# Pooling of k and v by halvings, and a new order for the first 750 of 2,051 pieces

## The chip, the core and the metric

The kernel runs on one core of a Trainium2 chip. Its time is the device time of one execution, in microseconds (us). A core has a matrix engine (PE, whose weight loads are listed apart as PEld), a vector engine (DVE), an activation engine (ACT) and a general engine (POOL); each works through a queue of its own, in order. SP is the queue that issues the DMA transfers.

## What is computed

Attention over keys and values that are averaged by eight, then a block that turns the result by learned angles and mixes it over tokens and channels. Eight batches, eight heads of 64, 576 tokens:

```python
k_p = k.reshape(B, H, Sp, pool, D).mean(axis=3)      # B=8 H=8 S=576 D=64 pool=8 Sp=72
v_p = v.reshape(B, H, Sp, pool, D).mean(axis=3)
scores = scale * np.matmul(q, k_p.transpose(0, 1, 3, 2))
attn = np.exp(scores - scores.max(-1, keepdims=True))
attn = attn / (np.sum(attn, axis=-1, keepdims=True) + 1e-09)
x = (attn @ v_p) as [8, 576, 512]
theta = x @ w_theta
zr, zi = x * np.cos(theta), x * np.sin(theta)
y = np.einsum('ts,bsd->btd', w_tok_r, zr) + np.einsum('ts,bsd->btd', w_tok_i, zi)
u = x + y
out = u + np.maximum(u @ w_ch, 0.0)
```

## The kernel before

Everything is float32; matrix products that need it are done as three products of a high and a low part ("h" and "l" at the end of a name), so most operands are first cast (`zh`, `xh`, `WTh`) and then subtracted (`zl`, `xl`, `WTl`).

The work is written as some 470 generators, called streams, and a long string, SCHEDULE, that says in which order they are advanced by one piece each. A word of the string is the name of a stream, and at its end, where there is a choice, the engine of that piece: v for DVE, g for POOL, a for ACT. Since each engine works through its queue in order, this string sets the order on all of them. There are 2,051 words. Per batch b the streams are: k and v (load a part of k or v), K and V (pool that part, and with no part number lay out the result as `kpT` or `Vh`, `Vl`), Q (queries, transposed into `qT`), S (scores, softmax; `en` is the normed exponent), E (its transposition), X (attention output, into `xT`), T (the angles: `pt` is x times w_theta, then sine and cosine, into `z`), Z (cast and split z, into `zh` and `zl`), M (token mix, into `py`, added to `xT`) and F (channel product `pf` and the output). At the start come h (w_theta), w and W (token weights: convert, then transpose by PE from `wt` into `WTh` and `WTl`) and c (w_ch, into `chh` and `chl`). The weights arrive as float64 and are converted by `to_f32`: three scalings, a combination on DVE at L366, and an addition on POOL at L368.

One pooling adds, for every pooled key or value, eight rows of 64 numbers. A part j = 0 or 1 of k or v is a tile of 128 partitions by 1024 numbers (`kpst`, `vpst`), the part j = 2 one of 64 by 512 (`kprst`, `vprst`). Batch 0 is pooled by matrix products on PE. From batch 1 on, `pool_sum` does it, on DVE by one reduction (L471), on POOL by halvings: the first half plus the second, three times, until 64 numbers are left (on POOL an operation of 512 numbers or more is cut in two by `InHalves`, L190). The large tiles `kpst`, `vpst` and `wcts` of the converted w_ch share one buffer, so that the next part can be loaded only when the last is pooled. The first 750 words put 11 pools on DVE: K1.0, K1.1, V1.0, K1.2, V1.1, K2.2, V1.2, K2.0, V2.2, V2.1, V3.2. Later in the string come four more on DVE: V4.1, K5.0, V6.2, K7.1.

After the change the lines behind the removed branch have numbers lower by four.

Of the kernel before, what the change touches and what calls it, by code (L numbers as in the profile page):

```python
# [35 lines left out]
w1.0a S0.2 w1.1v X0.0.0 w1.0v X0.0.1 X0.0.3 w1.1a W0a w1.1v S0.2a Q1.0 X0.0.1a w1.0 S0.4 w1.1 S0.3 W0 Q1.1 Q1.0
X0.0.0a S0.4 w1.1v X0.0.2 w1.0g S0.3g X0.0.2v X0.0.3v T0.0g T0.1g Q1.1a k1.1 w2.0 K1.1v W1 w2.0a S0.4 T0.0v W0 S0.3g
w2.0v W1a T0.1g S0.3 Q1.0a S0.2 W1 T0.0 w2.1 S0.4v w3.0 S0.3a K1 v1.0 w2.1v w3.0v w2.0a w2.1a T0.0 S0.2a w2.0 T0.1
w3.1 Q1.2 W1 w2.1a S0.4v T0.0 K1a S0.3 S0.3a S0.4 k1.2 S0.4a S0.4 Q1.3 V1.0v S0.4a T0.0 W0a w2.1 w3.0v T0.1 T0.1 w3.1a
X0.2.1 K1.2v X0.2.2 w3.0v w3.1v T0.0 X0.2.3 w2.0g X0.2.2a W1a W0 w3.1v T0.0a X0.2.0 T0.0 w4.0 v1.1 w2.1g w3.1 w3.0  # L40
w3.1g Q1.4 T0.0 X0.2.1v W2 T0.0 X0.2.3a Q1.2 w4.0v V1.1v Q1.3 X0.2.0a T0.2g T0.1 T0.1 w4.0a T0.2v T0.1a W2a c0 T0.2
Q1.3a w4.0a W2 T0.3g X0.2.3g T0.1 T0.3g T0.2 c0a T0.1 T0.3 w3.0g Q1.2v W2 T0.2 T0.4g T0.1 T0.2 c0a W1 w4.0 c1 T0.2
T0.4g T0.3 W2v T0.2a T0.2 c0a T0.2 W2 T0.4 w4.0g T0.3 T0.3 T0.2 T0.3 T0.4 W3 c0 Q1.4 T0.3a c0g c0g T0.4 T0.3 T0.4 T0.3
T0.4 c0g W3a T0.4 T0.3 W4 W3 T0.4 K1 Z0.0g K1a c1a S1.0 c1a W4a W4 c1a S1.0 c1 M0.0.0 W4a W4 Z0.1g Q1.4v c1v Z0.0v c1v
Z0.1v S1.0 M0.1.0 W4a W4 M0.0.0 M0.0.0 k2.2 M0.1.0 c2 W3 M0.1.0 W4a S1.0 c1v W4 S1.0g K2.2v c2a W3a W3 v1.2 M0.0.0
S1.0g S1.1 c2a c2a S1.1 S1.0 S1.1 M0.0.1 c2 S1.0v S1.0 c2g V1v S1.0 M0.0.1 M0.0.1 c2v c3 c2v S1.0a M0.1.1 S1.1 c3a
V1.2v S1.1g S1.1g S1.0 V1g c3a Z0.2a c3v S1.2 S1.2 M0.1.1 M0.1.0 S1.1 V1 v2.2 S1.3 M0.0.1 c3 c3g M0.2.0 c3v M0.2.0
M0.1.1 Z0.2v V1g S1.1a S1.1 M0.2.0 c3v M0.1.0a M0.1.1 Q2.0 S1.2 S1.1 k2.0 S1.1a M0.2.0 S1.4 S1.2 V1g Z0.3g M0.2.1
S1.2a S1.1 Q2.0 X1.0.0 X1.0.0v S1.2v X1.0.2 X1.0.1 X1.0.1a X1.0.3 X1.0.3v M0.2.1 S1.3 Z0.3g S1.2 X1.0.2a T1.0g T1.0g
S1.2a M0.0.1g M0.2.0v K2.0v M0.0.0v M0.2.1 M0.2.1 S1.2 T1.0 Q2.0 M0.2.0g S1.2 S1.3 S1.3 S1.2a S1.4 S1.3g k2.1 S1.3g  # L50
V2.2v T1.0 M0.3.0 M0.3.0 M0.1.1a Q2.1 S1.3 K2.1g S1.2 S1.4 T1.0 M0.3.1 S1.3v S1.3 M0.2.1v M0.0.1v M0.0.0g S1.3 M0.3.1
S1.3a K2 M0.2.1g S1.4 M0.3.0 S1.4g T1.1v k3.2 K2a M0.3.1 S1.3 T1.0 M0.3.0 M0.3.1 S1.4v T1.0 K2 M0.3.1g S1.4 Q2.1 v2.0
T1.0a K2v S1.4v S1.4 T1.1g Q2.1 T1.0 S1.4 T1.0 T1.1 S2.0 T1.0 S1.4a S1.4 V2.0g X1.2.2 T1.1 T1.1 M0.1.1g M0.3.0a v2.1
X1.2.0 X1.2.2a M0.3.1g X1.2.1 M0.1.0g S2.0 X1.2.3 T1.1 T1.1 Q3.0 X1.2.0a X1.2.3v M0.3.0v X1.2.1a T1.1v S2.0 T1.2g
F0.0.1 T1.2v T1.1 X1.2.3g S2.0 K3.2g T1.2 S2.0g T1.1 T1.1 S2.0g S2.1 V2.1v T1.3a Q3.0 T1.2 T1.3g T1.2 F0.0.1 S2.1
F0.0.0 S2.0 F0.0.0 T1.2 T1.3 F0.1.1 T1.4g F0.0.1 T1.2 F0.0.0 F0.1.0 S2.1 k3.0 K3.0g T1.2a S2.1 T1.2 T1.2 T1.2 T1.4v
S2.1g V2a F0.1.0 S2.1v k3.1 F0.2.0 T1.3 T1.3 F0.1.1 S2.2 S2.1 T1.3 T1.3 V2g T1.3v F0.0.1 E2.0 T1.3 S2.2 E2.0 S2.4 T1.3
S2.2 T1.3 S2.2 T1.4 T1.4 K3.1g T1.4 E2.0 F0.2.1 S2.3 T1.4 T1.4 F0.1.1 v3.0 T1.4 F0.2.0 F0.3.1 F0.1.0 F0.3.0 T1.4 Q3.0
Z1.0a Z1.1g F0.3.1 S2.2a F0.2.1 S2.2v E2.0 F0.3.0 K3 S2.3 K3a S2.3 M1.1.0 Z1.1v Z1.0g Q3.1 M1.0.0 E2.0a S2.3 M1.0.0
M1.0.1 M1.0.0 V2 S2.2 V3.0g M1.0.0 M1.0.0a F0.3.1 S2.3v M1.0.1 E2.0a V2g M1.0.1 F0.3.0 M1.1.1 S2.3v E2.0g E2.0g M1.1.0  # L60
S2.4 M1.0.1 M1.1.0 F0.1.1 F0.2.1 V2g Q3.1 v3.2 S2.4 K3 S2.4 S2.3 K3a F0.2.0 F0.3.1 Q3.1 M1.1.1 Z1.3g M1.1.1 S2.4a
M1.0.1a X2.0.0 S2.4g M1.1.0 X2.0.1 S2.4 X2.0.3 X2.0.0a v3.1 X2.0.2 X2.0.1a Z1.2a Z1.3v S3.2 X2.0.3a S3.2 S3.3 X2.0.2a
T2.0g T2.0v M1.3.0 E2.2 S3.2 S3.2 S3.2v M1.1.0v Z1.2g T2.0 T2.0 E2.2 E2.2 M1.2.1 T2.0 T2.1a S3.2v M1.2.1 T2.0 M1.1.1
S3.3 V3.1g M1.1.0v M1.2.1 T2.0 E2.2 M1.2.0 S3.4 M1.2.0 S3.0 V3.2v S3.3 M1.2.1 M1.1.1g S3.3 M1.0.1g M1.3.1 T2.1v S3.2
M1.2.0 M1.2.1v E2.2a E2.2g E2.2g E2.2g S3.3a M1.3.1 S3.3v k4.2 M1.2.0 S3.4 M1.2.0a k4.0 M1.3.1 M1.1.1g K4.2g M1.3.0
X2.2.2 M1.3.1 T2.0a S3.4 M1.3.0 S3.3 F0.2.1 X2.2.2a S3.4 T2.0 S3.4v M1.3.0 X2.2.0 S3.4g M1.2.1g X2.2.3 Q4.0 S3.4
X2.2.1 M1.2.0g S3.0 S3.1 X2.2.0a S3.0 M1.3.1a Q4.0 T2.0 T2.0 M1.3.1v V3g X2.2.3a v4.2 V3v K4.0g X2.2.1a T2.1 F1.0.1
T2.1 S3.0 M1.0.0g M1.3.0a E3.2 T2.2g F1.1.1 T2.1 F1.0.1 F1.2.1 V3 E3.2 T2.2g T2.3a M1.3.0g T2.1 Q4.0 F1.1.1 T2.1 V3v
F1.0.0 T2.1v F1.0.1 F1.0.0 F1.1.0 F1.0.0 T2.2 F1.2.1 S3.0a k4.1 E3.2 S3.0g F1.1.0 E3.2 K4.1g T2.1 T2.3g T2.1 K4 F1.2.0
T2.1 E3.2g S3.1 E3.2a F1.1.0 T2.2 S3.1 E3.2g F1.1.1 F1.3.0 E3.2g T2.2 Q4.1 K4a T2.2 Q4.1 F1.3.1 T2.2 V3g S3.0 T2.2a  # L70
S3.1 F1.3.0 F1.2.0 K4 T2.2 Q4.1 T2.2 K4a F1.0.1 T2.2 F1.3.1 F1.3.0 F1.3.1 T2.3 T2.3 T2.3 F1.1.1 F1.2.1 F1.2.0 X3.2.2
X3.2.3 X3.2.3a X3.2.1 S3.1g X2.2.3g X3.2.0 S4.2 X3.2.2v T2.3 X3.2.1v V4.2g X3.2.0a T2.3 S3.1v X3.2.3v T2.3a T2.4g
T2.4g S4.0 S3.1 T2.3 T2.3 T2.4 T2.3 T2.4 Z2.0v S4.0 T2.4 v4.0 T2.4 Z2.0g T2.4 Q5.0 F1.3.1 Z2.0g Z2.0g T2.4a E3.0 T2.4
M2.0.0 T2.4 T2.4 S4.0 Z2.1a S4.0 E3.0 S4.1 M2.0.1 Z2.1v E3.0 V4.0g M2.0.1 E3.0 M2.0.1 Z2.0g M2.0.0 Z2.0g S4.0a M2.0.0
S4.0v M2.0.0 M2.0.1 M2.1.0 M2.1.1 S4.1 M2.0.0 E3.0a E3.0g E3.0g M2.1.1 Z2.3a E3.0v M2.0.1 M2.1.1 M2.1.0 M2.1.0 M2.1.1
S4.0 X3.0.3 Z2.3g Z2.2a X3.0.0 X3.0.2 v4.1 X3.0.3a M2.3.0 V4.1v M2.1.0 M2.3.0 S4.1 X3.0.1 M2.3.0 X3.0.1v Z2.2g M2.2.0
S4.1 X3.0.2v M2.3.0 S4.1g k5.0 X3.0.0a k5.2 T3.4v Q5.0 S4.1v S4.3 T3.0g T3.0g S4.2 M2.2.0 S4.1 V4a T3.0 K5.0v T3.2a
S4.2 T3.0 k5.1 T3.1v T3.1g M2.2.0 T3.0 M2.1.0v M2.1.1a T3.1 M2.2.0 T3.0 F1.2.1 K5.2g E4.0 M2.3.1 T3.0 M2.3.1 S4.2
T3.0a M2.1.0v T3.0 M2.2.0a S4.2g S4.2v T3.0 v5.2 M2.0.0a M2.2.1 M2.3.1 T3.0 T3.2g T3.1 S4.4 M2.1.1v M2.3.0v T3.1 K5.1g
T3.1 M2.2.1 E4.0 E4.0 M2.2.0v E4.0 V4g T3.2 M2.0.0g M2.3.0g T3.1 S4.3 M2.0.1a T3.1a T3.1 T3.3a S4.3 T3.1 M2.3.1 T3.1  # L80
# [1164 lines left out]
```

## Time and profile before

| what | value |
|---|---|
| median of 3 runs | 562.17 us (560.41 to 565.18) |
| the profiled execution | 560.23 us |
| its span | 558.4 us |
| clock granted to PE, mean over the span | 0.993 of full |
| PE busy, PEld busy | 541.2 us, 511.7 us |
| DVE, ACT, POOL busy | 457.6, 331.8, 355.7 us |

The span is the time from the first to the last instruction that the profile shows; the execution's own time has 1.8 us around it. A matrix instruction is a weight load (PEld) and a product (PE), and loads run ahead under products. Both are shown, and in a stretch where PE has work all the time PEld is busy all the time too.

### The profile page before, as it was taken

What the parts mean: (1) busy time and instruction counts of PE and PEld (TensorE: products, weight loads), DVE (VectorE), ACT (ScalarE), POOL (GpSimd) and SP (SyncE); (2) the same over time, 40 slices, a digit from 0 to 9 for tenths busy, and PEclk for the clock granted to TensorE, in tenths of its full rate; (3) what the DMA queues carried; (4) which work ended last, traced back from release to release, by engine and by line L of the source; (5) the groups of instructions that cost most, each with busy time, mean ns of one, the idle gap of its engine ahead of it and who ended that gap; (6) DMA issues with size and microseconds to landing.
All of it is one profiled execution on the core that took longest, in us unless ns stands there. A gap on an engine that the chain in (4) does not pass through costs nothing.

```text
span 558.4 us, 11489 instructions
## 1 busy us (share of the span) xinstructions
PE 541.2 (97%) x4031; PEld 511.7 (92%) x4031; DVE 457.6 (82%) x850; ACT 331.8 (59%) x757; POOL 355.7 (64%) x497
## 2 busy tenths in 40 slices
...
GB/s 272 248 290 203 95 49 79 135 119 112 97 137 132 130 127 101 118 88 111 95 118 129 100 147 76 60 78 120 43 50 103 70 45 1 63 29 22 0 24 127
DMA packets 231802, 57.84 MB, mean 104 GB/s; under 512 B 218689, under 2 KB 220353, under 8 KB 231745
## 3 DMA queue, kind: packets, MB, share of 16 engines
...
## 4 chain that ended last, share of the span: by engine, by line
PE 66%; DVE 15%; ACT 8%; issue 4%; SPq 2%; DMA 2%; POOL 2%; DVEq 0%; POOLq 0%; ACTq 0%
PE py L1031 29%; PE pf L1064 12%; PE pt L943 11%; PE s L701 4%; PE pv L896 4%; PE px L957 2%; SPq L851 1%; PE warm L309 1%; DMA eraw<-G 1%; DVE zl L1015 1%; ACT L756 1%; DVE g L951 1%; DVE wsrc_a L366 1%; PE kpp L548 1%; PE vpp L548 1%
## 5 line engine op out<-in xcount | busy, mean ns | idle before, releaser
L1031 PE MATMUL py<-WTl,zh 128*128 128x288 f32 x576 | 82.8, 289 | 0.0
L1031 PE MATMUL py<-WTh,zh 128*128 128x288 f32 x576 | 81.3, 289 | 0.6 <-POOL zh L207 0.6
L1031 PE MATMUL py<-WTh,zl 128*128 128x288 f32 x576 | 81.2, 289 | 0.6 <-DVE er L819 0.5
L1031 PEld LDWEIGHTS py<-WTh,zl 128*128 128x128 f32 x576 | 74.7, 189 | 1.6 <-PE pe L797 0.7
L1031 PEld LDWEIGHTS py<-WTh,zh 128*128 128x128 f32 x576 | 74.4, 189 | 1.1 <-POOL zh L207 0.8
L1031 PEld LDWEIGHTS py<-WTl,zh 128*128 128x128 f32 x576 | 75.0, 190 | 0.3
L190 POOL TENSOR_TENSOR zl<-z,zh 128x256 fp32r<-128x256 f32 (+2 forms) x68 | 54.3, 829 | 27.3 <-ACT zh L205 14.6
L1041 DVE TENSOR_TENSOR xT<-py,xT 128x288 f32<-128x288 f32 x64 | 28.1, 447 | 28.4 <-PE py L1031 28.2
L949 ACT ACTIVATE g<-pt,c_magic 128x512 f32<-128x512 f32 x35 | 24.0, 685 | 45.4 <-PE pt L943 30.2
L190 POOL TENSOR_TENSOR ul<-xT,uh 128x288 fp32r<-128x288 f32 x40 | 33.2, 846 | 17.6 <-ACT uh L205 13.6
L1064 PE MATMUL pf<-uh,chh 128*128 128x288 f32 x256 | 43.7, 293 | 0.2 <-DVE z L983 0.2
L1064 PE MATMUL pf<-uh,chl 128*128 128x288 f32 x256 | 41.9, 287 | 0.0
L1064 PE MATMUL pf<-ul,chh 128*128 128x288 f32 x256 | 41.9, 286 | 0.0
L701 PE MATMUL s<-kpT,qT 128*128 128x144 f32 x256 | 38.5, 297 | 2.5 <-DVE WTl L435 1.4
L943 PE MATMUL pt<-th,xh 128*128 128x512 f32 x148 | 39.7, 391 | 0.4 <-DVE xT L1071 0.3
L943 PE MATMUL pt<-th,xl 128*128 128x512 f32 x148 | 38.1, 380 | 1.4 <-DVE xl L937 1.4
L701 PEld LDWEIGHTS s<-kpT,qT 128*128 128x128 f32 x256 | 35.0, 198 | 3.4 <-DVE WTl L435 1.6
L943 PE MATMUL pt<-tl,xh 128*128 128x512 f32 x148 | 38.0, 380 | 0.0
L190 POOL TENSOR_TENSOR xl<-xT,xh 128x256 fp32r<-128x256 f32 x40 | 29.6, 760 | 12.0 <-ACT xh L205 7.8
L1064 PEld LDWEIGHTS pf<-uh,chh 128*128 128x128 f32 x256 | 36.0, 190 | 1.0 <-PE pf L1064 0.4
L756 ACT ACTIVATE e_eps<-e_eps 128x576 f32<-128x576 f32 (+1 forms) x30 | 20.5, 685 | 27.5 <-DVE e_eps L752 27.3
L1064 PEld LDWEIGHTS pf<-uh,chl 128*128 128x128 f32 x256 | 35.6, 189 | 0.0
...
## 6 DMA issues: line engine op xcount, KB each, us to landing
...
```

What stands on the lines that cost most here:

```text
L190: nc.gpsimd.tensor_tensor(out[:, r], a[:, r], b[:, r], op)
L309: nc.tensor.matmul(p[:, 0:P], ident, ident, start=True, stop=True)
L548: nc.tensor.matmul(main[:, 2 * j : 2 * j + 2, :], ident, st[:, :, D * r : D * r + D], **steps[r])
L701: nc.tensor.matmul(scs[c // 2][:n, 2 * SP * (c % 2) : 2 * SP * (c % 2 + 1)], qT[:, c, t0 : t0 + n], kpT[:, c, :], start=True, stop=True,)
L756: nc.scalar.activation(e[:n], e[:n], AF.Exp, scale=scale)
L896: nc.tensor.matmul(as_written(pv[:, :gn]) if pair else pv[:, :gn], l, by_turns(r) if pair else r, start=i == 0, stop=i == len(terms) - 1,)
L943: nc.tensor.matmul(as_written(pt), l[:, c, :], by_turns(r[:, c, :]), start=i == 0, stop=i == 11)
L949: nc.scalar.activation(halves(g), in_order(pt), AF.Identity, bias=c_magic)
L957: nc.tensor.transpose(px[:, P * c : P * c + P], xT[:, c, o], ident)
L1031: nc.tensor.matmul(as_written(py[:, :n]), l[:, kk, :], by_turns(r[:, kk, t]), start=i == 0, stop=i == 3 * NK - 1,)
L1041: nc.vector.tensor_tensor(halves(u), in_order(py[:, :n]), halves(u), ALU.add)
L1064: nc.tensor.matmul(as_written(pv[:, :n]), l[:, kk, o], by_turns(uhl[r][:, kk, t]), start=i == 0, stop=i == 11,)
```

## The change

First, the branch of `pool_sum` that did a pooling on DVE by one reduction is gone, so that a pooling on DVE is three additions, of 512, 256 and 128 numbers in each partition for a large part and of 256, 128 and 64 for a small one. Second, the first 750 words of SCHEDULE stand in a new order, and some have another engine. The other 1,301 words are the same.

```diff
 SCHEDULE = """
-k0.0 w0.0 w0.0a k0.1 k0.2 D Q0.0 K0.0 w0.0v K0.1 w0.0g K0.0v h0 h1 w0.0 Q0.2 Q0.0 K0.1v K0 K0a K0.2 K0.2a Q0.0v h0v
...
@@ -466,10 +466,6 @@
     def pool_sum(t, width, dst, fine):
         w = width // 2
         e = pick()
-        if e == "v" and not fine:
-            by_pool = "p (r d) -> p d r" if len(t.shape) == 2 else "p c (r d) -> p c d r"
-            nc.vector.tensor_reduce(dst, t.rearrange(by_pool, d=D), AX.X, ALU.add)
-            return
         while w > D:
             ENG[e].tensor_tensor(t[..., 0:w], t[..., 0:w], t[..., w : 2 * w], ALU.add)
             if fine:
```

Of the 11 pools on DVE in the first 750 words, two stay there (K1.0 and K1.1), one comes (K4.2, from POOL), and nine go to POOL: V1.0, V1.1, K2.0 and V2.1 of the large ones, K1.2, K2.2, V1.2, V2.2 and V3.2 of the small ones. The four later ones stay on DVE, by halvings.

On DVE, at the angles of batch 0 while the token weights are converted (`wsrc_a`), before:

```order
L776 TENSOR_TENSOR en_4_563<-e_eps,ri_4_528 64x64
L951 SCALAR_TENSOR_TENSOR g_0_579<-g_0_579,pt_0_547 128x512
L471 TENSOR_REDUCE vp_622<-vpst_0_572 128x128
L366 SCALAR_TENSOR_TENSOR wsrc_a<-wsrc_a,chl_st 128x576
L357 TENSOR_SCALAR wsrc_b<-chh_st 128x576
L951 SCALAR_TENSOR_TENSOR spare<-spare,pt_1_583 128x512
L471 TENSOR_REDUCE kpr_639<-kprst_616 64x64
L364 TENSOR_SCALAR chh_st<-wsrc_a 128x576
L357 TENSOR_SCALAR wsrc_b<-chl_st 128x576
```

and after the change, at the like place:

```order
L903 TENSOR_SCALAR xT_461<-pv_0_1_470 128x256
L435 TENSOR_TENSOR WTl<-wt_0_450,WTh 128x8x128
L470 TENSOR_TENSOR kpst_1_436<-kpst_1_436 128x2x256
L470 TENSOR_TENSOR kpst_1_436<-kpst_1_436 128x2x128
L475 TENSOR_TENSOR kp_284<-kpst_1_436 128x128
L352 TENSOR_SCALAR wsrc_a<-wraw_0_447 128x576
L357 TENSOR_SCALAR wsrc_b<-wraw_0_447 128x576
L756 RECIPROCAL ri_3_523<-sm_3_391 128x8
L933 TENSOR_TENSOR xl_0_514<-xT_461,xh_0_513 128x512
```

One pooling of v and one of the small part of k have left this stretch of DVE's queue; the second large part of k is pooled here, by three additions.

On POOL, up to the last converted token weights (`wsrc_a` at L368) and the first of w_ch (`wcts`), before:

```order
L368 TENSOR_TENSOR wsrc_a<-wsrc_a,wsrc_b 128x576 x3
L207 CAST xh_2_700<-xT_451 128x512
L207 CAST xh_3_731<-xT_451 128x512
L207 COPY xr_734<-xT_451 128x4x64 x2
L190 TENSOR_TENSOR xl_3_732<-xT_451,xh_3_731 128x256 x2
L1178 MEMSET wpow 128x512
L368 TENSOR_TENSOR wsrc_a<-wsrc_a,wsrc_b 128x576
L207 CAST xh_4_764<-xr_734 128x512
L190 TENSOR_TENSOR xl_4_765<-xr_734,xh_4_764 128x256 x2
L368 TENSOR_TENSOR wsrc_a<-wsrc_a,wsrc_b 128x576
L368 TENSOR_TENSOR wcts_742<-wcts_742 128x512
L207 CAST chh<-wcts_742 128x512
```

and after:

```order
L368 TENSOR_TENSOR wsrc_a<-wsrc_a,wsrc_b 128x576 x2
L190 TENSOR_TENSOR vpst_0_599<-vpst_0_599 128x256 x2
L190 TENSOR_TENSOR vpst_0_599<-vpst_0_599 128x2x128
L190 TENSOR_TENSOR vp_625<-vpst_0_599 128x128
L368 TENSOR_TENSOR wsrc_a<-wsrc_a,wsrc_b 128x576
L190 TENSOR_TENSOR kprst_346<-kprst_346 64x256
L190 TENSOR_TENSOR kprst_346<-kprst_346 64x128
L190 TENSOR_TENSOR kpr_688<-kprst_346 64x64
L190 TENSOR_TENSOR vpst_1_650<-vpst_1_650 128x256 x2
L190 TENSOR_TENSOR vpst_1_650<-vpst_1_650 128x2x128
L190 TENSOR_TENSOR vp_625<-vpst_1_650 128x128
L368 TENSOR_TENSOR wsrc_a<-wsrc_a,wsrc_b 128x576
```

Three poolings (V1.0, K1.2, V1.1) now stand between the weight additions; the casts and splits of x (`xh`, `xl`) have gone to other engines.

On ACT, around the last of the angles of batch 0 and the first softmax of batch 1 (the table load and what follows), before:

```order
L205 CAST WTh<-wt_0_813 128x8x128
L989 ACTIVATE sn_4_841<-g_4_811,c_half 128x512
L205 COPY kpT<-pkr_856 64x64
L350 ACTIVATE wcts_862<-wcraw_776 128x512
L355 ACTIVATE wcts_862<-wcraw_776 128x512
L205 CAST WTh<-wt_848 128x4x64
L362 ACTIVATE wpow<-wcts_862 128x512
L740 ACTIVATE mx_0_873<-mx_0_873 128x8
L205 CAST WTh<-wt_848 128x4x64
L744 ACT_TABLE_LOAD
```

and after:

```order
L985 ACTIVATE sn_4_848<-g_4_823,c_half 128x512
L205 COPY kpT<-pkr_851 64x64
L350 ACTIVATE wcts_866<-wcraw_827 128x512
L205 CAST zh_0_868<-z_642 128x1152
L205 CAST zh_1_879<-z_642 128x1152
L205 CAST WTh<-wt_858 128x4x64
L205 COPY qT_425<-pq_4_843 128x4x64
L736 ACTIVATE mx_0_898<-mx_0_898 128x8
L740 ACT_TABLE_LOAD
L740 ACTIVATE e_eps,sm_0_900<-s_0_874,mx_0_898 128x72 x8
```

The casts `zh` of batch 0's first two channel blocks, which POOL did, and a copy of `qT`, which DVE did, now stand on ACT ahead of the softmax.

## Rows read from the trace of the kernel before

**Rows 1.** the page's first part, busy time, share of the span, instructions
```profile
PE 541.2 (97%) x4031; PEld 511.7 (92%) x4031; DVE 457.6 (82%) x850; ACT 331.8 (59%) x757; POOL 355.7 (64%) x497
```

**Rows 2.** busy time by stretch: PE, PEld, DVE, ACT, POOL, clock, DMA share, GB/s
```profile
20.00:77.40 57.40, 50.33 (x316) 39.60 (x315) 53.93 (x91) 50.65 (x145) 35.39 (x41) 0.97 0.72 182
77.40:182.40 105.00, 103.84 (x813) 99.28 (x812) 97.11 (x180) 80.72 (x234) 77.59 (x109) 1.00 0.56 108
182.40:558.40 376.00, 370.29 (x2803) 357.37 (x2801) 297.49 (x559) 190.77 (x349) 232.35 (x333) 1.00 0.47 81
14.30:17.70 3.40, 3.39 (x16) 2.98 (x14) 2.76 (x6) 2.68 (x10) 1.27 (x1) 0.50 1.09 319
```

**Rows 3.** the chain that ended last from 20 to 77.4, by line
```profile
by line: issue 18.4%; PE vpp L548 6.7%; DVE WTl L435 6.0%; DVE wsrc_a L366 5.8%; ACT spare L744 4.4%; PE s L701 3.9%; DVE wsrc_a L352 3.7%; DVE xl L937 3.1%; POOL chl L190 2.6%; DVE wsrc_b L357 2.6%; DVE wcts L366 2.3%; POOL wsrc_a L368 2.3
```

**Rows 4.** the chain from 160 to the end, by line
```profile
by line: PE py L1031 41.0%; PE pf L1064 17.0%; PE pt L943 15.2%; PE pv L896 5.5%; PE s L701 4.7%; PE px L957 2.5%; issue 1.7%; ACT en L765 0.9%; DVE sm L758 0.7%; DVE g L951 0.7%; PE s L693 0.7%; DVE G L785 0.6%; DVE xT L1071 0.6%; DMA out_
```

**Rows 5.** what PE waited for from 20 to 77.4: total, times, longest
```profile
PE wt L427 <- POOL wsrc_a L368: 1.5, 1, 1.5
```

**Rows 6.** DVE by line and form, 0 to 182.4: busy us, mean ns
```profile
L1041 DVE TENSOR_TENSOR xT<-py,xT 128x288 f32<-128x288 f32 x15 | 6.5, 444 | 0.5 <-PE py L1031 0.2
...
L471 DVE TENSOR_REDUCE kp<-kpst 128x128 f32<-128x1024 f32 x3 | 5.9, 1975 | 0.0
L471 DVE TENSOR_REDUCE vp<-vpst 128x128 f32<-128x1024 f32 x3 | 5.9, 1968 | 0.0
...
L937 DVE TENSOR_TENSOR xl<-xT,xh 128x512 fp32r<-128x512 f32 x5 | 5.1, 1014 | 0.4 <-POOL xh L207 0.4
...
L1015 DVE TENSOR_TENSOR zl<-z,zh 128x512 fp32r<-128x512 f32 x5 | 3.5, 702 | 0.0
...
L471 DVE TENSOR_REDUCE vpr<-vprst 64x64 f32<-64x512 f32 x3 | 3.1, 1022 | 0.0
...
L207 DVE COPY qT<-pq 128x512 f32<-128x512 f32 x4 | 2.7, 682 | 0.1
...
L769 DVE TENSOR_TENSOR en<-e_eps,ri 128x512 f32<-128x512 f32 x2 | 1.6, 809 | 0.0
...
L435 DVE TENSOR_TENSOR WTl<-wt,WTh 128x128 fp32r<-128x128 f32 x4 | 1.1, 274 | 0.0
```

**Rows 7.** POOL by line and form, the same stretch
```profile
L368 POOL TENSOR_TENSOR wsrc_a<-wsrc_a,wsrc_b 128x576 int32<-128x576 int32 x9 | 13.4, 1492 | 17.0 <-DVE wsrc_a L366 10.6 <-DVE ri L760 6.4
...
L207 POOL CAST zh<-z 128x1152 fp32r<-128x1152 f32 x5 | 6.1, 1236 | 4.9 <-DVE z L991 4.9
```

**Rows 8.** ACT by line and form, the same stretch
```profile
L205 ACT CAST zh<-z 128x1152 fp32r<-128x1152 f32 x3 | 3.4, 1147 | 1.0 <-DVE z L991 1.0
...
L205 ACT COPY qT<-pq 128x512 f32<-128x512 f32 x4 | 2.3, 586 | 0.0
```

**Rows 9.** POOL's timeline from 108: start, length; one pooling of k
```profile
108.43 2.22 POOL L190 TENSOR_TENSOR kpst<-kpst 128x256 f32<-128x256 f32 x3
110.73 0.46 POOL L190 TENSOR_TENSOR kp<-kpst 128x128 f32<-128x128 f32 x1
```

**Rows 10.** the tile vpst from 40 to 62: its four loads, issue to landing
```profile
DMA to landing us min/median/max: 4.1/4.7/5.2
```

**Rows 11.** DVE's timeline at 75.5 and at 84.4, the same operation
```profile
75.50 1.33 DVE L366 SCALAR_TENSOR_TENSOR wcts<-wcts,wpow 128x512 int32<-128x512 int32 x1
...
84.44 0.67 DVE L366 SCALAR_TENSOR_TENSOR wcts<-wcts,wpow 128x512 int32<-128x512 int32 x1
```

**Rows 12.** POOL's timeline at 74
```profile
74.05 2.23 POOL L207 CAST zh<-z 128x1152 fp32r<-128x1152 f32 x2 [1.11 <-DVE z L991]
```

**Rows 13.** POOL's timeline at 66.6
```profile
66.64 1.42 POOL L368 TENSOR_TENSOR wsrc_a<-wsrc_a,wsrc_b 128x576 int32<-128x576 int32 x1 [1.17 <-DVE wsrc_a L366]
```

**Rows 14.** PE's timeline at 71 and at 75, the last weights and the first mix
```profile
71.15 0.71 PE L427 MATMUL wt<-ident,wsrc_a 128*128 128x128 f32 x5
...
75.25 1.00 PE L1031 MATMUL py<-WTh,zh 128*128 128x288 f32 x6 [0.56 <-POOL zh L207]
```

More of the change, by code (lines that the diff above doesn't have):

```diff
@@ L36 @@
[L36 to L80, printed above, removed]
@@ L131 @@
[L131 to L135 removed]
+w0.0 w0.0v k0.2 k0.0 k0.1 w0.0a D w0.0a K0.0 K0.1 w0.0 h0 K0.2 K0.0a h0a Q0.0 h0v K0.1a Q0.0 Q0.2 h0v w0.0 K0 h0 h1
@@ new lines @@
+X0.0.3 K1.1v w1.0 w2.1 w1.1 X0.0.0a W1 w2.0v X0.0.3a T0.0g S0.2a T0.1a w2.0v W0 S0.3 S0.3g T0.0v W1a W1 w2.0v Q1.1
+S0.4 Q1.1a S0.2 W0a w2.1a w3.0 Q1.0 T0.1v S0.3g w2.0 T0.0 w3.1 Q1.0a W1 S0.3 S0.2a S0.4v w2.1a w2.1a T0.1 w4.0 T0.0
+S0.4g v1.0 T0.0 w3.1a w2.0 S0.3v w3.1a S0.3 w2.1 S0.4 S0.3a w2.1 S0.4a S0.4 w3.0v Q1.3 W1v S0.4a V1.0g W1 Q1.2 T0.0
+w3.0v T0.1 w3.1a W0 T0.0 X0.2.2 T0.0a X0.2.2v T0.1 v1.1 W2 X0.2.3 w3.1 w3.1 w4.0a K1 T0.0 X0.2.0 w3.0a T0.0 X0.2.3v
+K1v T0.0 X0.2.1 X0.2.0a K1.2g Q1.2 Q1.3 T0.1 X0.2.1v T0.2v T0.2v T0.1 T0.3a w3.0 T0.2 X0.2.3a w4.0a c0 T0.1v T0.3v
```

158 lines of the change are left out of this document (99 added, 59 removed).

## The prediction

> **What bounds the kernel now.** I read first the busy times [rows 1]: PE 97%, PEld 92%, DVE 82%. Over the whole, PE bounds. But a share is an average over stages, so next come the stretches [rows 2], cut where the token mixes start (77.4) and where the pieces begin that the change leaves alone (182.4). PE counts as busy while a product waits for operands in its pipeline, so I read PEld: a stretch in which PE has all the work it can take has PEld busy throughout. From 182.4 on it is busy 357.37 of 376.00, from 77.4 to 182.4 it is 99.28 of 105.00, and from 20 to 77.4 only 39.60 of 57.40. So the time to be won in the part that the change touches is at most 17.8 us in the one stretch and 5.7 us in the other. In the first, DVE is busy 53.93 of 57.40 (94%) and ACT 50.65 (88%), POOL 35.39 (62%). Then the chain of waits: in that stretch it goes over DVE, ACT, POOL and issue, with PE in short pieces [rows 3]; from 160 on it is PE, with 41% in the mixes alone [rows 4]. So **until 77 us DVE is the bound, ACT close behind it; from there to 182 PE mostly, with DVE at 92% (97.11 of 105.00) just behind; then PE.** PE's own waits in the first stretch are few; one of 1.5 us is for token weights that POOL adds at L368 [rows 5].
>
> The change must thus be priced by what it takes off DVE's queue ahead of the first mix, and by what it puts on ACT and POOL for it.
>
> **A pooling on DVE.** A reduction takes 1.97 us for a large part and 1.02 for a small one [rows 6]. No trace of before shows halvings on DVE. Their nearest rows are additions of the same size with both inputs in SBUF: 512 numbers 0.70 (zl), 288 numbers 0.44 (xT), 128 numbers 0.27 (WTl), so 256 numbers lie between the last two and I take 0.42. A large part then is 0.70 + 0.42 + 0.27 = 1.4 us, 0.6 less than the reduction; a small part (256, 128, 64 numbers) 0.42 + 0.27 + 0.2 = 0.9, an estimate, about 0.1 less. The bound the other way is the same addition when it is held up: the 512-number operation at L366 takes 0.67 alone, and 1.33 while POOL casts zh [rows 11, 12]. With the two larger steps at double, a large part costs 2.5 us, 0.5 more than the reduction.
>
> **A pooling on POOL.** The one at 108 took 2.22 for its first three operations and 0.46 for the last [rows 9], 2.7 us together; a small part, three operations of half the size, I put at 1.5. So each of the nine pools that move frees 2.0 or 1.0 us of DVE for 2.7 or 1.5 of POOL. Until 77 POOL has 22 us idle in this stretch.
>
> **Until the first mix (term 1).** By the order on each engine, ahead of the first mix DVE had four large poolings and one small (4 x 1.97 + 1.02 = 8.9 us) and has two large ones by halvings (2.8): 6.1 off. Four copies of qT go to ACT: 4 x 0.68 = 2.7 off. On come two en from POOL, 2 x 0.81 = 1.6, and three xl from POOL, 3 x 0.70 to 1.01 = 2.1 to 3.0 [rows 6] (the lower price is that of zl, which has the same size), and small copies for kpT and WTh which I count at 1. The sum is 3.1 to 4.1 off; I take 4, because the xl row's mean contains held-up ones. At 94% busy that is worth at most 3.8 us. Against it ACT gets the four qT (4 x 0.59 = 2.3) and two zh (2 x 1.15 = 2.3) [rows 8], less about 0.7 of small exchanges: 3.9 us on. ACT had 57.40 - 50.65 = 6.75 idle there, of which not all can be used: the two zh and the last qT stand late, ahead of the softmax of batch 1. So ACT takes DVE's place as the bound before DVE's relief is used up. Of the 3.8 I take 1.5, nearer to zero than to the whole because ACT's queue at the place where the mix is awaited is the longer one by 2.3. Bounds: 0 and 3.8.
>
> **From 77 to 182 (term 2).** Here six pools leave DVE (K2.0, V2.1 at 1.97, K2.2, V1.2, V2.2, V3.2 at 1.02: 8.0) and K4.2 comes at 0.9. What DVE takes over from the other two engines eats most of the rest; counted over both queues with the durations of the rows, 2.2 to 4.6 us come off by the end of the stretch (the spread is that of the place at which I stop counting). PE is short of loads only 5.7 us there, not all for DVE. I take 1.5, half of the middle, because PE is the bound for most of this stretch; bounds 0 and 4.4 (4.6 at 95%).
>
> **The other 1,301 words.** Four pools on DVE become halvings: two large at 0.6 less (V4.1, K5.0), two small at nothing to 0.1 less. They lie beside a PE that is busy 95% with loads [rows 2, 4], so their worth is 0; the cover is the mixes' matrix work. If DVE's additions there are held up, they cost 0.5 each, which PE's work hides as well. The order there is unchanged, and what is loaded, too. The SP queue's loads in the first part are moved but the same in number; a load of a large v part takes 4.7 us to land [rows 10], and the next may only come when the buffer has been pooled.
>
> **The sum.** 1.5 + 1.5 = 3.0 us off. The profiled execution, 560.23 (a span of 558.4 and 1.8 around it), becomes 557.2; the median of the runs, 562.17, becomes 559.2. The profiled execution is the fastest of those shown, so the middle of a new set will lie nearer the median: I say **558.5**, 0.65% below the median. About 1%, 5.6 us, is what a measurement of this kernel can tell from no change.
>
> **A rule that speaks against the change.** The trace shows that DVE's operations with two inputs last up to twice as long while POOL works [rows 11, 12], where the reductions show means within 1% of each other, 1975 and 1968 ns [rows 6]. The Trainium skill (SBUF — State Buffer, Who interferes with whom) says why: a DVE instruction with two inputs in SBUF and a POOL instruction that reads SBUF exclude one another for a whole instruction, and tensor_reduce never contends. By that rule, the trace agrees with it, each pooling put on POOL adds blocked time to both queues, and halvings on DVE add some that reductions did not have.
>
> **Rivals.** *A: the relief counts in full.* DVE is the bound in both stretches and ACT's extra work falls into its idle time: 3.8 in the first and 2.2 to 4.4 in the second, 6.0 to 8.2 in all, 554.0 to 556.2. For it: DVE at 94% and 92%. Against: ACT at 88%, and the 5.7 us cap. *B: the relief is eaten*, by ACT as the new bound and by exclusion: nine pools bring some 31 operations to POOL; if a third of them meet a two-input operation of DVE (such operations fill about a third of its time, an estimate from its groups) and cost it 0.4 us (over half of the 0.66 by which the [rows 11] differ), that is 4.1 us on a queue that was to gain 4 + 2.2. Then 560 to 563. For it: those rows. Against: POOL gives up other work that excluded DVE too. *C, slower: POOL's queue is late with the token weights.* Before, its last addition at L368 of these weights ended at 68.06 [rows 13] and PE transposed the last of them at 71.15 [rows 14]: 3.1 us to spare. Now V1.0, K1.2 and V1.1 stand in that queue among the weight additions: 2.7 + 1.5 + 2.7 = 6.9 us where xh, xl and xr stood with some 5. Each of the three also waits for its load, and the two v parts share a buffer: 4.7 + 2.7 for each where it was 4.7 + 2.0. With 1.9 more work, 1.4 of later loads, and 0.4 of blocking on some eight operations (3.2), the addition would come 6.5 later, 3.4 beyond the spare time, and the mixes start as much later; DVE's relief doesn't help, since DVE waits for POOL. If PE then pauses, it can have another stretch at half clock like the one at 14.3 (3.4 us at 0.50, [rows 2]; there is a second one at 24.5), 1.7 us each. 562.2 + 3.4 + 1.7 = 567.3, with two stretches 569. It decides from the point where the last L368 of these weights lands more than 3.1 us later than now. Against: the additions waited for DVE (17.0 us idle ahead of nine of them, [rows 7]), and a lighter DVE sends its part earlier. *D: it does not do what it says*, because the pools were covered all the time; then 561 to 563, as B.
>
> **How the numbers follow.** Forecast 0.40 (556.6 to 561), A 0.25, B with D 0.22, C 0.13. Faster by over 1% (below 556.5): nearly all of A and a little of the forecast, 0.27. Slower by over 1% (above 567.8): most of C, 0.11. Within 1%: the rest, 0.62. The range leaves out the far ends of A and C: 551.5 to 567.
>
> **What would show it.** Right: the first mix starts 1 to 2 us before its 75.25 of now [rows 14], DVE less than 94% busy in the stretch before, ACT above 88%, PEld's idle time until 182 shorter by 3 us, and the stretch from there to the end as long as before, 376 us to within 1. Halvings on DVE at 0.70, 0.42 and 0.27. B: the same first mix time, ACT ending the waits. C: PE waiting for POOL's L368, a later first mix, more half-clock stretches. The forecast is wrong if the last 376 us change by more than 2, since no term is written for it.

## The result, and the profile after

The changed kernel takes 565.74 us (median of 20 runs, 562.58 to 569.61), the kernel before 562.17 (20 runs, 560.0 to 568.21): a ratio of 1.0057, with an interval from 1.0031 to 1.0083. It is slower by some 3.2 us by this ratio (the medians are 3.6 apart), where 558.5 had been predicted. In a later set on one chip the same two stood at 567.07 (6 runs) and 562.07 (1.0087, 1.0064 to 1.0109), 5.0 us apart. Here and below a median is taken over all executions of a kernel, while a ratio leaves out those more than 1.5% above its fastest.

The profiled execution took 563.64 us, with a span of 561.5. Busy times of the whole, by engine:

```profile
PE 541.7 (96%) x4031; PEld 511.3 (91%) x4031; DVE 450.8 (80%) x871; ACT 338.1 (60%) x767; POOL 350.6 (62%) x494
```

and by the stretches of [rows 2], with the columns PE, PEld, DVE, ACT, POOL, granted clock, DMA share and GB/s:

```profile
20.00:77.40 57.40, 49.01 (x288) 37.76 (x289) 51.81 (x96) 52.13 (x147) 33.18 (x37) 0.92 0.68 177
77.40:182.40 105.00, 104.35 (x818) 100.10 (x818) 92.86 (x183) 83.67 (x241) 73.33 (x110) 1.00 0.54 110
182.40:561.50 379.10, 371.89 (x2812) 358.40 (x2811) 297.58 (x571) 192.63 (x353) 233.57 (x333) 1.00 0.48 81
```

DVE did lose about what the prediction counted in sum: 53.93 to 51.81 us until 77.4, 97.11 to 92.86 until 182.4, 6.4 us together. ACT gained 1.5 and 3.0. PE has not gained from it: until 77.4 its loads are busy 37.76 us where they were 39.60, and its clock there is 0.92, not 0.97. In PE's timeline of the changed kernel (start, length, engine, line, operation, and in brackets what ended an idle time) the places to compare are these:

```profile
22.23 0.63 PE L793 MATMUL pe<-ident,en 128*128 128x128 f32 x4 [2.39 <-DVE en L765]
...
27.25 1.23 PE L689 MATMUL s<-kpT,qT 64*64 64x72 f32 x16 [1.19 <-ACT qT L205]
28.40 2.18 PE L697 MATMUL s<-kpT,qT 128*128 128x144 f32 x8
...
30.85 4.05 PE L544 MATMUL vpp<-early,ident 128*128 128x128 f32 x32
...
35.28 1.04 PE L427 MATMUL wt<-ident,wsrc_a 128*128 128x128 f32 x8
...
73.51 0.74 PE L427 MATMUL wt<-ident,wsrc_a 128*128 128x128 f32 x5 [0.97 <-DVE WTl L435]
...
74.64 2.19 PE L697 MATMUL s<-kpT,qT 128*128 128x144 f32 x8 [0.39 <-DVE WTl L435]
...
76.94 0.85 PE L1027 MATMUL py<-WTh,zh 128*128 128x288 f32 x2
```

Before, the like rows of the start are

```profile
24.03 0.76 PE L693 MATMUL s<-kpT,qT 64*64 64x72 f32 x16 [2.15 <-ACT spare L744]
24.72 2.29 PE L701 MATMUL s<-kpT,qT 128*128 128x144 f32 x8
...
31.53 2.02 PE L548 MATMUL vpp<-early,ident 128*128 128x128 f32 x16
33.39 1.04 PE L427 MATMUL wt<-ident,wsrc_a 128*128 128x128 f32 x8
```

The scores of S0.4 (64 by 64, sixteen of them) come at 27.25 where they came at 24.03, the first token weights are transposed at 35.28 and not 33.39 (1.89 later), the last ones at 73.51 and not 71.15, and the first mix starts at 76.94 and not 75.25 [rows 14], 1.69 later. At the end of the new order, at the first pv of 182 us, PE is 1.07 late; at 207 us, in the part where the pieces are the same, 3.02:

```profile
206.97 0.76 PE L1060 MATMUL pf<-uh,chh 128*128 128x288 f32 x4 [1.30 <-ACT kpT L205]
```

The same product started at 203.95 before, with no wait. From there to the end the two run alike: PE's last product starts 2.69 later. So in this pair of executions the loss has two places, **the start (until 35 us) and the seam of the new order and the old (182 to 207 us)**; between them 0.2 us was won until the first mix and 0.6 behind it. Further profiles, set side by side in the part on the clock below, bear out the first place only.

### The profile page after: what moved, and what is told of

Its sections match the earlier page's. It is cut to its first block, busy times and chain, and to the rows that moved or that the text cites. A ratio compares the mean times of both kernels' runs of the same rounds, so it can differ in the third digit from the quotient of the medians.

```text
span 561.5 us, 11513 instructions
## 1 busy us (share of the span) xinstructions
PE 541.7 (96%) x4031; PEld 511.3 (91%) x4031; DVE 450.8 (80%) x871; ACT 338.1 (60%) x767; POOL 350.6 (62%) x494
## 4 chain that ended last, share of the span: by engine, by line
PE 75%; DVE 10%; ACT 6%; SPq 3%; issue 2%; DMA 2%; POOL 2%; DVEq 0%; POOLq 0%; ACTq 0%
PE py L1027 34%; PE pt L939 13%; PE pf L1060 12%; PE pv L892 6%; PE s L697 4%; SPq L847 3%; PE px L953 2%; DVE g L947 1%; DVE xT L1067 1%; DMA kpst<-in_k_dram 1%; POOL wsrc_a L368 1%; DVE G L781 1%; DVE mx L731 1%; ACT en L761 1%; PE kpp L544 1%
## 5 line engine op out<-in xcount | busy, mean ns | idle before, releaser
L190 POOL TENSOR_TENSOR zl<-z,zh 128x256 fp32r<-128x256 f32 (+2 forms) x64 | 51.4, 835 | 28.7 <-ACT zh L205 16.1
L205 ACT CAST zh<-z 128x1152 fp32r<-128x1152 f32 (+1 forms) x22 | 23.9, 1099 | 25.3 <-PE py L1027 20.3
```

Of the source, the lines that this page charges most:

```text
L190: nc.gpsimd.tensor_tensor(out[:, r], a[:, r], b[:, r], op)
L205: nc.scalar.copy(out, src)
```

## The experiments

**Which edit.** The halvings alone, in the old order:

```diff
-        if e == "v" and not fine:
-            by_pool = "p (r d) -> p d r" if len(t.shape) == 2 else "p c (r d) -> p c d r"
-            nc.vector.tensor_reduce(dst, t.rearrange(by_pool, d=D), AX.X, ALU.add)
-            return
```

> The kernel before with halvings in place of the reduction, in the old order: 15 poolings on DVE by halvings. If the loss of 3.2 us came from halvings on DVE that are held up by POOL, this kernel, which has eleven in the first part where the changed one has three, is slower than before by 3 us or more (0.6%). If the loss lies in the new order, this one is within 1 us of before, or faster by 1 to 2 us, since a large part should take 1.4 us and not 1.97 on the engine that bounds the first 77 us.

567.31 us against 561.88, a ratio of 1.0085 (1.0054 to 1.0117): 5.4 us slower. The halvings on DVE, by form, until 190 us (busy us, mean ns):

```profile
L470 DVE TENSOR_TENSOR vpst<-vpst 128x512 f32<-128x512 f32 x3 | 4.0, 1331 | 0.0
...
L470 DVE TENSOR_TENSOR vpst<-vpst 128x256 f32<-128x256 f32 x3 | 3.2, 1082 | 0.1
...
L470 DVE TENSOR_TENSOR kpst<-kpst 128x512 f32<-128x512 f32 x3 | 2.6, 875 | 0.2 <-DMA kpst<-in_k_dram 0.2
...
L470 DVE TENSOR_TENSOR kpst<-kpst 128x256 f32<-128x256 f32 x3 | 2.2, 718 | 0.1
...
L475 DVE TENSOR_TENSOR kp<-kpst 128x128 f32<-128x128 f32 x3 | 1.6, 526 | 0.1
...
L475 DVE TENSOR_TENSOR vp<-vpst 128x128 f32<-128x128 f32 x3 | 0.9, 317 | 0.1
```

A large part of v lasts 1.33 + 1.08 + 0.32 = 2.7 us where the reduction lasted 1.97 [rows 6], a large part of k 0.88 + 0.72 + 0.53 = 2.1, where 1.4 had been put. The worst place is one pooling of v. DVE's timeline, then POOL's, then PE's:

```profile
129.30 3.86 DVE L470 TENSOR_TENSOR vpst<-vpst 128x512 f32<-128x512 f32 x2
133.19 0.29 DVE L475 TENSOR_TENSOR vp<-vpst 128x128 f32<-128x128 f32 x1
133.40 0.68 DVE L947 SCALAR_TENSOR_TENSOR g<-g,pt 128x512 f32<-128x512 f32 x1
```

```profile
128.99 1.97 POOL L190 TENSOR_TENSOR en<-e_eps,ri 128x256 f32<-128x256 f32 x3
130.92 1.40 POOL L190 TENSOR_TENSOR xl<-xT,xh 128x256 fp32r<-128x256 f32 x2
132.28 0.60 POOL L207 CAST xh<-xr 128x512 fp32r<-128x512 f32 x1
```

```profile
134.14 1.23 PE L939 MATMUL pt<-th,xh 128*128 128x512 f32 x4 [2.24 <-DVE g L947]
135.16 1.91 PE L939 MATMUL pt<-tl,xh 128*128 128x512 f32 x4
```

Two additions that should last 0.70 and 0.42 last 1.50 and 2.32, 3.86 together. Beside them POOL goes from en to xl to xh without a gap; the second addition ends at 133.16, 0.28 after the end of that run (132.88). Behind them on DVE waits g, and for g PE waits 2.24 us. Some 1 us later the granted clock falls to half, and four products take 1.91 us that take 1.03 in the kernel before. Busy times of PE, PEld, DVE, ACT and POOL, granted clock, DMA share and GB/s there:

```profile
135.10:138.40 3.30, 3.30 (x9) 2.61 (x8) 3.20 (x8) 3.27 (x4) 0.98 (x2) 0.50 0.40 149
```

The reduction at the same place, while POOL did the same en and xl, took

```profile
126.15 1.98 DVE L471 TENSOR_REDUCE vp<-vpst 128x128 f32<-128x1024 f32 x1
```

The reverse of the edit, the new order with the reduction put back into `pool_sum`:

> The changed kernel with the reduction back: the new order alone. If the order is the cause, it is as slow as the changed kernel, within 1 us (565 to 566). If the halvings are, it is back at the time before, 562.

566.45 us, 1.0073 (1.0045 to 1.0102). This cannot be told from the changed kernel, so the new order alone is enough for the loss. In the changed kernel only three poolings of the first part are halvings on DVE, and they are short. The changed kernel's, until 190 us:

```profile
L470 DVE TENSOR_TENSOR kpst<-kpst 128x512 f32<-128x512 f32 x2 | 1.4, 677 | 0.0
...
L470 DVE TENSOR_TENSOR kpst<-kpst 128x256 f32<-128x256 f32 x2 | 1.1, 572 | 0.1
...
L475 DVE TENSOR_TENSOR kp<-kpst 128x128 f32<-128x128 f32 x2 | 0.6, 293 | 0.1
```

**The one place alone**, in the kernel before:

```diff
-        if e == "v" and not fine:
+        if e == "v" and not fine and not halve:
...
-        yield from pool_sum(st, POOL * D, dst, b == 0)
+        yield from pool_sum(st, POOL * D, dst, b == 0, (name, b, j) == ("vp", 2, 1))
```

> The kernel before with one pooling by halvings, that of V2.1, all others by reduction. In the run with halvings alone the two larger additions of this pooling lasted 3.86 us together beside POOL's en and xl, where the reduction lasted 1.98, and PE then waited 2.24 us for the g that stands behind it. If exclusion between DVE and POOL at such places makes halvings dear, this one edit costs 2 to 4 us of the 5.4. If the 5.4 us come from many small shifts, it costs less than 1 us.

566.84 against 562.98, 1.0071 (1.004 to 1.0102): 3.9 us, from one of the fifteen poolings on DVE. DVE's two additions, and PE's wait for g:

```profile
126.57 3.85 DVE L474 TENSOR_TENSOR vpst<-vpst 128x512 f32<-128x512 f32 x2
```

```profile
131.40 1.13 PE L943 MATMUL pt<-th,xh 128*128 128x512 f32 x4 [2.23 <-DVE g L951]
```

So by these medians most of the 5.4 us of the halvings is this one meeting of DVE and POOL. The wait of 2.23 us is not all of it: here too the granted clock is 0.50 a little later, from 132.5 to 135.9 us, where the kernel before has 1.00.

**The engine letters of the ten pools**, without the order. First the new order with the letters as before (`V1.0g` to `V1.0v` and so on, `K4.2v` to `K4.2g`, and the reduction):

> The new order with the engine letters of the ten moved pools as they were (nine on DVE, by reduction, K4.2 on POOL). If the poolings on POOL cause the loss (their loads wait for the one buffer and hold the SP queue, and they hold up DVE's additions), this is faster than the changed kernel by 2 to 3 us. If the order of the other pieces causes it (the stores of batch 0 left behind the transposing transfers in the SP queue, the casts before the first mix), it is as slow or slower, by up to 2 us, because DVE has 13 us more to do.

577.19 us, 1.0262 (1.0228 to 1.0296). Then the old order with the new letters, and halvings:

> The old order with only the engine letters of the ten pools changed, and halvings. If the poolings on POOL cause the loss, this kernel is slower than before by 3 us; if only the order of the rest does, it is as fast as before or faster by 1 to 4 us, since DVE, at 94% busy until 77 us and 92% after, loses 13 us of work.

574.99 us, 1.024 (1.0194 to 1.0286). Against the kernels with the same order and the same kind of pooling (the new order with reductions, 566.45, and the old with halvings, 567.31) the ten letters alone cost 10.7 and 7.7 us, more than either theory had. The order and the letters fit only together. A likely reason, which no run takes apart, is that the old order has POOL cast and split x where three poolings would come, while the new one has these casts elsewhere.

**The two queues that seemed late in the changed kernel.** Its SP queue was busy 16.3 of the 17.4 us from 165 to 182.4 with issues (as much as before), and its transfers for E3.2 were issued from 188.25, before from 185.83. One word moved, the stores of F0.3.1 ahead of the load of v3.1 (word 724 to place 666):

```diff
+F0.3.1 v3.1
...
-F0.3.1 S3.3a
+S3.3a
```

> The changed kernel with one word moved: the last piece of F0.3.1, four stores of batch 0, stands ahead of the load of v3.1 and the 16 transposing transfers of E2.2 in the SP queue, and not behind them. If the SP queue, which is busy 94% from 165 to 182, carries the lag of 2.5 us into the common part, this is 1 to 2.5 us faster than the changed kernel. If the lag there comes from DVE's or ACT's work of batch 3, it is the same within 0.7 us.

569.72 us, 1.0099 (1.0065 to 1.0134): not faster than the changed kernel. And POOL's timeline in the changed kernel had, with the addition of weights behind a pooling that waits for its load, and on DVE a long scaling beside that addition:

```profile
61.23 2.77 POOL L190 TENSOR_TENSOR vpst<-vpst 128x256 f32<-128x256 f32 x3 [1.79 <-DMA vpst<-in_v_dram]
...
64.83 1.42 POOL L368 TENSOR_TENSOR wsrc_a<-wsrc_a,wsrc_b 128x576 int32<-128x576 int32 x1
...
68.04 1.41 POOL L368 TENSOR_TENSOR wsrc_a<-wsrc_a,wsrc_b 128x576 int32<-128x576 int32 x1 [1.32 <-DVE wsrc_a L366]
```

```profile
65.07 2.00 DVE L364 TENSOR_SCALAR chh_st<-wsrc_a 128x576 f16<-128x576 f32 x1
```

(Two other scalings of that size take 0.48 and 0.60.) One word moved by two places, V1.1g behind the addition:

```diff
-V1.1g W2 w3.0
+W2 w3.0 V1.1g
```

> The changed kernel with one word moved by two places: the pooling V1.1 on POOL stands behind the addition of token weights (L368, third part) and not ahead of it. POOL idled 1.8 us for the load of that pooling with the addition waiting behind it, and the addition then held up a DVE scaling (2.00 us, not 0.46) that the next weights needed. If POOL's queue delays the mixes in this way, the first mix comes 1 to 2 us earlier and the kernel is faster by as much. If DVE or ACT bound the start otherwise, the time is the same within 0.7 us.

566.24 us, 1.0053 (1.0027 to 1.0078): no change that can be told. The addition now comes at 63.91, hardly earlier, and the last one at 69.92, later than 68.04, since it waited for DVE's part and not for POOL's queue:

```profile
63.91 1.54 POOL L367 TENSOR_TENSOR wsrc_a<-wsrc_a,wsrc_b 128x576 int32<-128x576 int32 x1 [3.00 <-DVE wsrc_a L365]
...
69.92 1.43 POOL L367 TENSOR_TENSOR wsrc_a<-wsrc_a,wsrc_b 128x576 int32<-128x576 int32 x1 [0.33 <-DVE wsrc_a L365]
```

Both together:

> Both words moved. If the two delays are the loss and add up, it is faster than the changed kernel by 2 to 4 us, and level with the kernel before (562). If only one of them counts, it is like the better of the two.

567.06 us, 1.0096 (1.006 to 1.0132). Neither theory of a late queue is borne out.

**The clock.** Each execution comes with its mean granted clock. What the lower clock took is put at (1 - clock) times the span. Over 102 executions of before it was 4.0 us on the mean, over 26 of the changed kernel 6.3; and within each of the two, executions with more of it took longer, by 0.69 and 0.71 us for each microsecond. In the changed kernel's profile it fell to half here:

```profile
23.80:30.40 6.60, 4.61 (x33) 3.82 (x32) 6.19 (x14) 6.54 (x33) 3.69 (x3) 0.50 1.06 204
74.60:78.20 3.60, 3.44 (x13) 3.13 (x14) 3.53 (x8) 3.46 (x7) 1.42 (x4) 0.53 0.09 13
```

one stretch longer than that of [rows 2], and one that falls on the scores ahead of the first mix and on the mix itself. The eight scores there take 2.19 us and not 1.25 as before. Ahead of the long one PE was idle more than before. Busy times from 20 to 28, the changed kernel first, then before:

```profile
20.00:28.00 8.00, 3.78 (x37) 3.00 (x39) 7.01 (x16) 7.90 (x37) 2.60 (x4) 0.72 1.05 277
```

```profile
20.00:28.00 8.00, 5.85 (x47) 5.13 (x46) 7.29 (x19) 7.77 (x40) 3.98 (x5) 0.79 1.08 197
```

To fill such waits, idle products were put in PE's queue, into banks that the next real products overwrite:

```diff
+    def fill(out, n):
+        for _ in range(n):
+            nc.tensor.matmul(out, ident, ident, start=True, stop=True)
...
         pt = bank([P, NC, P], f"pe{b}_{m}")
+        if (b, m) == (0, 0):
+            fill(pt[:, 0, :], 9)
```

> The changed kernel with 13 idle matrix products (identity by identity, 128 columns, into banks that the next real products overwrite) in two places where PE waits: nine ahead of the first transposition of en (a wait of 2.4 us), four ahead of the scores of S0.4 (1.2 us). They stand where PE has nothing else to do. If the stretch at half clock from 23.5 to 30.5 follows from PE's idleness between 19.8 and 27 and costs time, it becomes shorter, the mean granted clock rises from 0.989 to about 0.992, and the time falls by 1.5 to 3 us. If the clock is only a companion of late data, the clock rises and the time stays, or grows by up to 1 us.

564.5 us, 1.0022 (0.9988 to 1.0055, without 569.48 and 570.31 of the twelve); mean loss to the clock 5.4 us.

> The same with four more such products ahead of the first mix, where PE waits for zh. If the half clock at the start of the mixes (74.5 to 78.5) follows from that wait and costs time, it is up to 1.5 us faster than with the first 13 alone; otherwise equal to it, or slower by up to 1 us, the length of the products.

564.64 us, 1.0031 (1.0002 to 1.0059, without 570.5); mean loss to the clock 4.1 us. Its profiled execution, the shortest of the twelve, has a span of 558.5 us at a mean clock of 0.997.

> The changed kernel itself on the same chip, for comparison with the two that are filled: 565 to 566.5, 0.5 to 0.8% slower than before, with a median of (1 - granted clock) times span some 2 to 3 us above that of before.

567.07 us, 1.0087, on the same chip; mean loss to the clock 5.7 us. So 13 or 17 products that compute nothing make the changed kernel 2.5 us faster by these medians, and the intervals of both ratios lie below that of the changed kernel (1.0064 to 1.0109). With all 24 executions of the two filled kernels counted, their mean is 564.5, against 567.0 for the six here and 566.1 for all 26 of the changed kernel: a gain of 1.6 to 2.5 us, about half of the loss. The same in the kernel before:

> The kernel before with eleven such products in its own waits: four ahead of S0.1's scores, five ahead of the transposition of the last queries, two ahead of the first mix. If the clock at the start costs time, it loses one of its two half-clock stretches in most executions and is 1 to 2 us faster than before; if not, it is the same within 1 us.

561.74 us, 0.9986 (0.9964 to 1.0008). It lost only 1.4 us to the clock, not 4.0, and yet was not measurably faster. Its PE gets to the pooling of v early and then waits for the load:

```profile
31.57 2.02 PE L552 MATMUL vpp<-early,ident 128*128 128x128 f32 x16 [2.31 <-DMA early<-in_v_dram]
```

In the kernel before the same products start at 31.53, without this wait. So the old order has some 2.3 us of room here, and up to that much of what PE loses at half clock ahead of it costs nothing.

The profiles side by side (start of the instruction, us):

| | before | before, filled | changed | changed, second profile | changed, 17 fillings |
|---|---|---|---|---|---|
| first token weights on PE | 33.39 | 33.43 | 35.28 | 38.72 | 35.51 |
| first mix | 75.25 | 75.36 | 76.94 | 80.44 | 75.80 |
| first pv of 182 us | 182.37 | 182.61 | 183.44 | 186.37 | 181.74 |
| PE's last product | 553.97 | 556.78 | 556.66 | 560.35 | 554.60 |

From the first mix to the last product the old order takes 478.7 and 481.4 us, the new one 479.7, 479.9 and 478.8. So no loss behind the first mix is shown, and the seam of the first pair is within what executions differ by. The start does stand out. In all 13 profiles of the new order the first token weights come at 35.28 to 40.27. In the four of the old order with the pools where they were they come at 33.37 to 33.71, and in three of these PE waits 1.5 to 2.3 us for the load of v.

**What delays the start.** The chain of waits of the changed kernel from 14 to 40 us lies on ACT from 18 to 27, almost without a gap (start, length, what):

```profile
17.99 2.54 ACT e_eps L740 x16
...
20.75 0.71 ACT wsrc_b L355
21.47 0.47 ACT qT L205
21.93 0.77 ACT chl_st L362
...
22.78 2.54 ACT spare L740 x16
...
26.22 0.76 ACT chh_st L362
...
27.25 1.23 PE s L689 x16
```

Two runs of exponentials (S0.0, S0.1), and around them scalings of weights and copies of qT, some of which the old order had on DVE. Three pieces back to DVE:

```diff
-Q0.3a ... w0.1a ... h2a
+Q0.3v ... w0.1v ... h2v
```

> The changed kernel with three pieces of the start given back from ACT to DVE: a copy of qT (0.56 on ACT) and the scalings chl_st and chh_st (0.86 and 0.76), 2.2 us of ACT between 21 and 27 where it has no idle time and carries the chain. If ACT at the start is where the new order loses, the scores of S0.4 come at 25 to 25.5 and not at 27.25, the first transposition of token weights some 2 us earlier, and the kernel is 1.5 to 2.5 us faster than the changed one (564). If DVE is the bound there as the prediction had it, the 1.6 us more on DVE make it as slow or slower (566 to 568).

566.5 us, 1.0057 (1.0029 to 1.0085, without 571.98), no gain; mean loss to the clock 6.8 us. S0.4 came no earlier (28.52, in the changed kernel's two profiles 27.25 and 29.84), since en on DVE was later: PE waited 3.26 us for it, and 2.39 in both of those, with S0.4 behind:

```profile
24.11 1.09 PE L792 MATMUL pe<-ident,en 128*128 128x128 f32 x4 [3.26 <-DVE en L764]
...
28.52 1.23 PE L688 MATMUL s<-kpT,qT 64*64 64x72 f32 x16 [0.46 <-ACT qT L204]
```

With fillings:

> The same, with nine idle matrix products ahead of the first transposition of en and four ahead of the first mix, as in the run with 17 of them but without the four ahead of S0.4. If ACT's lateness and the clock both cost, this is the fastest of the new order, 561 to 563, level with the kernel before; if the lateness alone does and the clock only follows, it equals the run without them.

564.32 us, 1.0034 (1.0005 to 1.0064, without 571.43); 5.4 us lost to the clock. Then the order in PE's queue, three words moved in front of the transposition of en:

```diff
-S0.0 S0.2 v0.0 ... Q0.4 k1.2 h2 Q0.4a S0.1g h3 S0.2 S0.4
+Q0.4 Q0.4a S0.4 S0.0 S0.2 v0.0 ... k1.2 h2 S0.1g h3 S0.2
```

> The changed kernel with three words moved to the front of S0.0's transposition, so that PE's queue at 20 us has the order of the kernel before: the last queries' transposition and the scores of S0.4 stand ahead of pe of S0.0, which waits 2.4 us for en on DVE, and not behind it. If the place of these in PE's queue delays the start (the same wait stood there when ACT had less to do), the scores of S0.4 come at 23 to 24 and not at 27.25, the first transposition of token weights 2 us earlier than 35.28, and the kernel is 1.5 to 3 us faster than the changed one (563 to 564.5). If PE's order there doesn't matter, it stays at 565.5 to 567.

568.09 us, 1.0115 (1.0077 to 1.0154). The scores come earlier, and the first token weights do not come before 35.28:

```profile
25.49 1.22 PE L688 MATMUL s<-kpT,qT 64*64 64x72 f32 x16 [2.79 <-ACT qT L204]
...
36.95 1.04 PE L426 MATMUL wt<-ident,wsrc_a 128*128 128x128 f32 x8
```

Its executions lost 9.3 us to the clock on the mean.

> The same with six idle matrix products ahead of pe of S0.0 and four ahead of the first mix. If the clock still falls at the start and costs time, it is another 1 to 2 us faster (562 to 563); if the earlier scores alone keep PE busy, it equals the run without them.

564.95 us, 1.0049 (1.0018 to 1.008); 4.9 us lost to the clock. Filling takes some 3 us off here.

## Why the prediction was wrong

**DVE's relief: the amount was about right, its worth was not.** 6.0 to 8.2 us were to come off DVE; 6.4 did, though only 2.1 of them until 77.4, where about 4 had been counted, and 4.3 behind. The step that failed is "of the 3.8 I take 1.5", and behind it the reading that DVE is the bound until 77 us. The first mix was to come 1 to 2 us earlier; it came 1.69 later. The stretch from 20 to 77.4 is an average over stages with different limits. In its first quarter, until the token weights are first transposed, the new order's time hangs on batch 0's softmax, which goes over ACT, PE and DVE by turns in fixed orders. The old order waits there for a load of v, with room before it. There the new order is 1.9 us late (5.3 in its second profile), and the sum had no term for it. From the first transposition to the first mix, where DVE's relief lies, it takes 41.66 us (41.72 in the second profile) and not 41.86. So the relief brought some 0.2 us, not 1.5, and the late start came on top. With 17 fillings this part took 40.29, so the clock may have hidden some of the relief. Rival B had the engine right (ACT stands on the chain from 18 to 27) and said no change; giving ACT's work back did not bring the time back, so ACT alone is not shown to be the cause.

The room itself was read too simply. PEld is not busy throughout wherever PE has work: from 50.8 to 55.2 us in the kernel before PE does two products of pv in every 0.73 us without a wait, and its loads are busy 0.30 of that. So not all of the 17.8 us was to be won.

**The second term** was to bring 1.5. From the first mix to 182 us 0.6 came in the first pair of profiles, though the first mix stood at half clock there. I had put the cost of the later pieces at nothing, with the matrix work as its cover. In the first pair they took 378.1 us and not 376.0, just beyond the 2 us that the prediction itself named as a sign against it. But the kernel before with fillings also takes 378.3 there, so no run shows that the seam costs anything. The SP queue was 2.4 us late there, and the stores moved ahead did not bring time.

**Halvings on DVE** were put at 1.4 us for a large part, with 2.5 as the upper bound and the lower taken. They cost from 1.5 (the changed kernel's k: 0.68 + 0.57 + 0.29) to 4.1 (one v beside POOL: 3.86 + 0.29), above that upper bound. The rule of the Trainium skill that was cited against the change (SBUF — State Buffer, Who interferes with whom) is the right one: the trace agrees that a reduction lasts the same beside POOL (1.98) and that a two-input addition is held up beside POOL's instructions, in one case through a run of several (2.32 us). It made no difference to the result, since the new order keeps only three such poolings in the first part: with the reduction put back, the time is the same. The halvings cost 5.4 us in the old order. Whether the moved poolings and the new order avoid some of that is not shown: the changed kernel stood 3.6 and 5.0 us above the kernel before in its two sets.

**Rival C** (POOL late with the token weights, the mixes later, more half clock) had the right outcome, a later first mix and a stretch at half clock on it, and the wrong mechanism: the last addition ended at 69.45 and not 68.06, 1.4 later and within the 3.1 to spare, and taking the pooling out of its way changed nothing. That 565.74 lies inside the stated 551.5 to 567 is luck: the upper end was there for C.

**The clock** was in the prediction only as a supplement to C. It is a main term: 2.3 us more are lost to it, worth 1.6 us by the slope within each kernel (an estimate), and the fillings bring 1.6 to 2.5 us. It is not all: with 17 fillings the loss to the clock is that of before (4.1 and 4.0 us), and the kernel is still 0.3% slower. What piece makes the start late stays open: no single piece that was moved brought it back, and no run puts the old order's start ahead of the rest of the new order.

What the prediction had right: DVE at a lower share and ACT above 88% (52.13 of 57.40, 91%).
